# Gated attention on one core: the last MLP chunk's reads issued ahead of a load of x, and one gate value in another buffer

## The chip, the cores and the metric

The kernel runs on one core of a Trainium2 chip. A core has five engines that run side by side and wait for one another through semaphores: TensorE (matrix products, PE in the profile, its weight loads are PEld), VectorE (DVE), ScalarE (ACT), GpSimd (POOL) and SyncE (SP), which issues most of the DMAs. The metric is the time of one execution on the device in microseconds (us). Three executions of the kernel before took 1954.82, 1956.88 and 1960.61 us; the median is 1956.88.

## The reference

The input x has 2048 tokens of width 640. With a layer norm of it, attention and an MLP are computed side by side, and the MLP gates the attention:

```python
xn = layernorm(x)
q  = (xn @ wq)  per head                 # 32 heads of 128
p  = softmax(q @ k.T * 128**-0.5)        # the last 512 cached positions, no mask
s  = (p @ v, heads side by side) @ wo
h  = relu(xn @ w1 + b1) ** 2             # inner width 1728
g  = silu(h @ w2 + b2)
out = x + s * g
```

All arrays are float32, and the result has to be as exact as float32.

## The kernel before

**Products in three parts.** Each float32 operand is split into a high and a low part: ACT rounds a copy (`hi`), DVE or POOL subtracts (`lo`). A product is then three matmuls, high by high, high by low, low by high. In the profile a tile's split is a pair such as `ACT ACTIVATE ch<-ch` and `DVE TENSOR_TENSOR ch<-ch,ch`. A group of 15 matmuls is five such triples.

**Stages.** The tokens are cut into four tiles of 512. First comes the MLP: its inner width is 14 chunks (13 of 128 and one of 64). Tile 0 is done chunk by chunk; the first projections of tiles 1 and 2 are done next, and their activations are stored to DRAM as `h_m`. A loop over 28 steps then does the second projections of tiles 1 and 2, a chunk in each step (line 1275; steps 0 to 13 for tile 1, 14 to 27 for tile 2; below, chunk m is that of step m). The MLP of tile 3 is spread over the attention. Attention runs over 128 units (a token tile and a head each).

**One step of the loop.** `c_load(m + 3)` (line 764) reads a chunk's second weights (`cw`, 320 KB) and its activations (`ch<-h_m`, 256 KB) on SP's queue. `c_prep(m + 2, k)` (line 774) splits the activations (k = 0) and the weights (k = 1) on ACT and DVE. `c_down(m)` (line 801) is the step's 15 matmuls into five PSUM banks, `py`. The buffers are rings: four for raw weights (`wr`), four for raw activations (`tmp`), three for split weights, two for the split activations of odd steps. A tile that takes the next place in a ring waits for the last user of that place.

```python
for m in range(2 * FC):                      # line 1275, FC = 14
    t, f = CS[m]
    if m + 3 < 2 * FC:
        c_load(m + 3)
    if m + 2 < 2 * FC:
        for k in range(2):
            c_prep(m + 2, k)
    ...
```

**The border.** At step `OPEN` = 21 the attention's pool of tiles, `ep`, is opened, and the raw weights of head 0 (`qr`, `kr`) and the normalised x of the first token tile (`ax<-xT_d`, two DMAs of 1280 KB, high and low part) are read. At step 23 (`OPEN + 2`) head 0's weights are split, head 1's are read into the same single raw buffers, and the x of the second token tile is read into its own. At step 25 head 1's weights are split. At step 27, ahead of its 15 matmuls, TensorE does the first query projection (`pq`), which ACT and DVE turn into the first `q` value.

**The gate.** After the last step, `gate(T2, ...)` (line 520) makes tile 2's gate value from each of the five `py` banks: a sigmoid on ACT, a multiplication on DVE, and a store to DRAM on POOL's queue (`g_d<-sgl`). The function given to `gate` names the tile that holds the value. It is a tile of the tag `wv0` or `wv1`, in turn, the later home of the split v weights, each a ring of G = 2:

```python
gate(T2, lambda d: pools["ep"].tile([P, NT], F32, tag=f"wv{d % 2}", name=f"sgl{d}", bufs=G))
```

So values 0, 2 and 4 share the two places of `wv0`. TensorE meanwhile does 15 matmuls for tile 3 (`eu`), and then the first unit's scores (`s`, 12 matmuls), whose PSUM banks are those that `py` held. The scores of a unit are put at a fixed place in a block of 256 of TensorE's instructions (`align`, line 1373, first place 188), as are steps 4 to 20 of the loop (line 1315); padding instructions (NOP) fill up to it.

**The order of the work.** The code is unrolled. Instructions of PE, DVE, ACT, POOL and SP are in general kept in the order in which the code writes them on each engine, so what stands ahead on a queue and waits holds up what stands behind. From the attention's first unit on, a plan sorted by due times writes that order.

**Names in the profile.** Nearly every operation is recorded by one helper, so it shows line L77; the tile names tell them apart: `cw`, `ch` (second projection), `qr`, `kr`, `ax`, `pq`, `q` (query), `sgl`, `g_d` (gate), `eu` (tile 3's early projection), `s` (scores).

Of the kernel before, what the change touches and what calls it, by code (L numbers as in the profile page):

```python
# [8 lines left out]
F32 = mybir.dt.float32  # L9
# [5 lines left out]
P = 128  # L15
NT = 512
# [9 lines left out]
def kernel(  # L26
# [20 lines left out]
    DC = D // P  # L47
    FC = (F + P - 1) // P
    KC = W // P
    LATE = NTILE - 1  # L50
    OPEN = 2 * FC - 7
    SCALE = DH**-0.5
    G = 2
# [46 lines left out]
    T1, T2 = 1, 2  # L100
# [102 lines left out]
    def ln_chunk(t, c):  # L203
        if c == 0:
            open_x(t)
        bc, xs = LN[t], XS[t]
        xc = (
            pa.tile([P, D], F32, tag="xb", name=f"xc{t}_{c}", bufs=NB)
            if t == T2 and c in (1, 3)
            else xp.tile(  # L210
                [P, D], F32, tag="mr" if t == T2 and c == DC - 1 else "stage", name=f"xc{t}_{c}"
            )
        )[:, :NT]
        nc.sync.dma_start(xc, xT[c * P : (c + 1) * P, t * NT : (t + 1) * NT])
        dve.tensor_tensor(xc, xc, bc[0], op=ALU.subtract)
        dve.tensor_tensor(xc, xc, bc[1], op=ALU.mult)
        XC[t, c] = xc

    def ln_split(t, c, k):
        xc, xs = XC[t, c], XS[t]  # L220
        if k == 0:
            act.activation(xs[0][:, c, :], xc, AF.Copy)
        else:
            dve.tensor_tensor(xs[1][:, c, :], xc, raw(xs[0][:, c, :]), op=ALU.subtract)
# [135 lines left out]
    def spill(t, xs, cs=slice(0, DC)):  # L360
        for i in range(2):
            pool.dma_start(xT_d[t][i][:, cs, :], raw(xs[i])[:, cs, :])
# [144 lines left out]
    XS, HS, PY, LN, XC, WR, SUMS, TS, WB, PB, pools = ({} for _ in range(11))  # L507
# [12 lines left out]
    def gate(t, tiles, ds=range(DC)):  # L520
        for d in ds:
            py = PY[t][d]
            sg = tiles(d)
            act.activation(sg, py, AF.Sigmoid, bias=b2_sb[:, d : d + 1])
            dve.scalar_tensor_tensor(
                sg, py, b2_sb[:, d : d + 1], sg, op0=ALU.add, op1=ALU.mult
            )
            pool.dma_start(g_d[t][:, d, :], sg)
# [11 lines left out]
    def tmp(name):  # L540
        return xp.tile([P, NT], F32, tag="tmp", name=name, bufs=4)
# [222 lines left out]
    def c_load(m):  # L764
        t, f = CS[m]
        f0, n = chunks[f]
        r = xp.tile([P, D], F32, tag="wr", name=f"cw{m}", bufs=4)
        for i in range(0, P, n):
            sp.dma_start(r[i : i + n, :], w2[f0 : f0 + n, :])
        h = tmp(f"ch{m}")  # L770
        sp.dma_start(h[:n, :], h_m[t, f][:n, :])
        WR["c", m, 1], WR["c", m, 0] = r, h

    def c_prep(m, k):
        n = chunks[CS[m][1]][1]
        src = WR.pop(("c", m, k))
        if k:
            hi, lo = WB["c", m, 1] = [
                pc.tile([P, D], F32R, tag=f"w2{i}", name=f"cw{m}_{i}", bufs=3) for i in range(2)
            ]  # L780
        else:
            hs = (
                h_tiles(f"ch{m}")
                if m % 2
                else [
                    pc.tile([P, NT], F32R, tag="r", name=f"ch{m}_{i}", bufs=4) for i in range(2)
                ]
            )
            WB["c", m, 0] = hs[0] if n < P else hs
            hi, lo = (hs[0][:n, :], hs[0][n : 2 * n, :]) if n < P else hs  # L790
            src = src[:n, :]
        act.activation(hi, src, AF.Copy)
        dve.tensor_tensor(lo, src, raw(hi), op=ALU.subtract)
# [3 lines left out]
    def lead_slot(m):  # L797
        passes = sum(2 * (2 if chunks[CS[k][1]][1] < P else 3) * DC for k in range(LEAD_STEPS[0], m))
        return (MID_SLOT + passes + LEAD_PADS * (m - LEAD_STEPS[0])) % BLOCK

    def c_down(m):
        t, f = CS[m]
        if f == 0:
            PY[t] = [ps_y.tile([P, NT], F32, tag="py", name=f"py{t}_{d}") for d in range(DC)]
        down(f, WB.pop(("c", m, 1)), WB.pop(("c", m, 0)), PY[t])
# [14 lines left out]
    AHEAD = 2  # L820
# [12 lines left out]
    def open_xT(hf, t):  # L833
        XT[hf, t] = [
            pools["ep"].tile(
                [P, DC, NT], F32R, tag=f"x{i}", name=f"ax{hf}_{t}_{i}", bufs=TPH
            )
            for i in range(2)
        ]

    def load_xT(hf, t, i, cs, queue=sp):
        queue.dma_start(raw(XT[hf, t][i])[:, cs, :], xT_d[hf * TPH + t][i][:, cs, :])
# [12 lines left out]
    def load_raw(kind, hf, h):  # L855
        r = raw_tile(kind, f"{kind}r{hf}_{h}")
        src = {"q": wq, "k": kT, "v": v}[kind][h] if kind != "o" else wo[h * DH : (h + 1) * DH]
        if kind in "qv":
            r = r.rearrange("p (c d) -> p c d", d=DH)
        sp.dma_start(r, src)  # L860
        RAW[kind, hf, h] = r

    def prep(kind, hf, h, eng=None):
        shape = {"q": [P, DC, DH], "k": [P, W], "v": [P, KC, DH], "o": [P, D]}[kind]
        home = {"q": WQ, "k": KT, "v": VV, "o": WO}[kind]
        hi, lo = home[hf, h] = pair(f"w{kind}", shape, f"w{kind}{hf}_{h}", 2 * G if kind == "o" else G)
        src = RAW.pop((kind, hf, h))
        act.activation(hi, src, AF.Copy)
        (eng or pool).tensor_tensor(lo, src, raw(hi), op=ALU.subtract)

    def q_mm(i, cs):
        hf, g, t, h = units[i]
        if 0 in cs:
            QPS[i] = bank(f"pq{i}", 1)
        ws, xs = WQ[hf, h], XT[hf, t]
        for c in cs:
            triple(
                QPS[i],
                (ws[0][:, c, :], ws[1][:, c, :]),
                (xs[0][:, c, :], xs[1][:, c, :]),  # L880
                c == 0,
                c == DC - 1,
            )

    def q_hi(i):
        Q[i] = pair("q", [P, NT], f"q{i}", AHEAD + 1)
        act.activation(Q[i][0], QPS[i], AF.Copy, scale=SCALE)

    def q_lo(i):
        dve.scalar_tensor_tensor(  # L890
            Q[i][1], QPS.pop(i), SCALE, raw(Q[i][0]), op0=ALU.mult, op1=ALU.subtract
        )
# [381 lines left out]
    bctx.close()  # L1274
    for m in range(2 * FC):
        t, f = CS[m]
        if m + 3 < 2 * FC:
            c_load(m + 3)
        if m + 2 < 2 * FC:
            for k in range(2):  # L1280
                c_prep(m + 2, k)
        c, odd = divmod(m - 2, 2)
        if not odd:
            if 0 <= c < DC:
                ln_chunk(LATE, c)
                for k in range(2):
                    ln_split(LATE, c, k)
            if 0 < c <= DC:
                spill(LATE, XS[LATE], slice(c - 1, c))
        if m == OPEN:  # L1290
            pools["ep"] = ctx.enter_context(tc.tile_pool(name="early", bufs=1, side="right"))
            load_raw("q", 0, 0)
            load_raw("k", 0, 0)
            open_xT(0, 0)
            for i in range(2):
                load_xT(0, 0, i, slice(0, DC))
        if m == OPEN + 2:
            for kind in "qk":
                prep(kind, 0, 0, dve)
                load_raw(kind, 0, 1)  # L1300
            open_xT(0, 1)
            for i in range(2):
                load_xT(0, 1, i, slice(0, DC))
        if m == OPEN + 4:
            for kind in "qk":
                prep(kind, 0, 1, dve)
        if m == 2 * FC - 1:
            hctx.close()
            pools["psa"] = ctx.enter_context(
                tc.tile_pool(name="psa", bufs=1, space=PSUM, side="right")  # L1310
            )
            q_mm(0, range(DC))
            q_hi(0)
            q_lo(0)
        if m in LEAD_STEPS:
            pe.addr_align(BLOCK, lead_slot(m))
        c_down(m)
        if m == FC - 1:
            gate(T1, gate_tile)
    gate(  # L1320
        T2,
        lambda d: pools["ep"].tile([P, NT], F32, tag=f"wv{d % 2}", name=f"sgl{d}", bufs=G),
    )
    EARLY_IN = (-1,) * 5 + (0,) * 4 + (1,) * 4 + (2,) * 4 + (3,) * 3
    EARLY = [(FA + n // DC, n % DC) for n in range(len(EARLY_IN))]
    for (f, c), u in zip(EARLY, EARLY_IN):
# [127 lines left out]
    for item in order:  # L1454
        kind, n = item[0], int(item[1:] or 0)
# [125 lines left out]
```

## Time and profile before

| | |
|---|---|
| median of three executions | 1956.88 us |
| the profiled execution: time, span | 1955.08 us, 1953.3 us |
| TensorE busy | 1943.1 us (99%), 8576 matmuls |
| VectorE, ScalarE, GpSimd busy | 1599.5, 1242.6, 1348.2 us |
| granted TensorE clock | 0.999 |
| DMA traffic | 246.43 MB, mean 126 GB/s |

The span runs from the first to the last instruction of the profiled execution; its time has some 2 us around it. A row of a timeline gives start, length, engine, line, operation, tiles (output, arrow, inputs), shape and count; in brackets the idle time of the engine before it and what ended it. A row of the chain of waits gives start, length and what the end of the kernel waited for in that stretch. A row of waits gives who waited for whom, the total in us, how often, and the longest. A row of a stretch gives its bounds and length, the busy time of each engine (with the number of instructions), the granted clock, and the share and rate of the DMA engines. SPq and PEldq are the instruction queues of SyncE and TensorE.

### The profile page before, as it was taken

What the parts mean: (1) busy time and instruction counts of PE and PEld (TensorE: products, weight loads), DVE (VectorE), ACT (ScalarE), POOL (GpSimd) and SP (SyncE); (2) the same over time, 40 slices, a digit from 0 to 9 for tenths busy, and PEclk for the clock granted to TensorE, in tenths of its full rate; (3) what the DMA queues carried; (4) which work ended last, traced back from release to release, by engine and by line L of the source; (5) the groups of instructions that cost most, each with busy time, mean ns of one, the idle gap of its engine ahead of it and who ended that gap; (6) DMA issues with size and microseconds to landing.
All of it is one profiled execution on the core that took longest, in us unless ns stands there. A gap on an engine that the chain in (4) does not pass through costs nothing.

```text
span 1953.3 us, 28587 instructions
## 1 busy us (share of the span) xinstructions
PE 1943.1 (99%) x8576; PEld 1605.8 (82%) x8576; DVE 1599.5 (82%) x2758; ACT 1242.6 (64%) x2150; POOL 1348.2 (69%) x729
## 2 busy tenths in 40 slices
PE   9999999999999999999999999999999999999998
PEld 7888878888888888888888888888888888888887
DVE  6864747788888888888888878888888888888864
ACT  5665536766666666666666676666666666666643
POOL 1022106888888888888888888888888888888841
PEclk9999999999999999999999999999999999999999
DMA  7557953333332233333335433443343333323253
GB/s 267 150 179 252 365 176 112 98 93 92 93 92 93 92 93 92 93 93 92 92 98 179 144 110 109 114 114 114 114 114 114 114 114 114 98 92 93 85 186 119
DMA packets 147639, 246.43 MB, mean 126 GB/s; under 512 B 25020, under 2 KB 47334, under 8 KB 146214
## 3 DMA queue, kind: packets, MB, share of 16 engines
q1 hardware_dynamic: 144486, 230.02, 38.6%
q0 software_dynamic: 2864, 14.42, 1.8%
q8 instruction: 77, 1.26, 0.2%
q14 instruction: 68, 0.56, 0.1%
q10 hardware_dynamic: 144, 0.16, 0.0%
HBM read 213.59 MB, written 30.95 MB: 125 GB/s over the span
## 4 chain that ended last, share of the span: by engine, by line
PE 97%; DMA 2%; DVE 0%; issue 0%; ACT 0%; SPq 0%; ACTq 0%; POOLq 0%; DVEq 0%
PE r L77 22%; PE pq L77 22%; PE s L77 18%; PE o L77 18%; PE py L77 6%; PE ph L77 2%; PE ly L77 2%; PE wa L77 2%; PE lu L77 2%; PE wy L77 1%; PE wx L77 1%; DMA w1r<-in_w_dram 1%; DMA ch<-h_m 1%; PE eu L77 1%; DMA xb<-in_x_dram 0%; DMA w2r<-in_w_dram 0%
## 5 line engine op out<-in xcount | busy, mean ns | idle before, releaser
L77 POOL TENSOR_TENSOR pt<-e,pt 128x1024 fp32r<-128x1024 f32 x256 | 615.6, 2405 | 113.1 <-ACT pt L77 69.5
L77 PE MATMUL r<-ot,wo 128*128 128x512 f32 x1920 | 496.6, 389 | 0.0
L77 PE MATMUL pq<-ax,wq 128*128 128x512 f32 x1920 | 456.1, 389 | 0.0
L77 PEld LDWEIGHTS pq<-ax,wq 128*128 128x128 f32 x1920 | 360.4, 188 | 75.2 <-DVE q L77 0.4
L77 PEld LDWEIGHTS r<-ot,wo 128*128 128x128 f32 x1920 | 360.5, 188 | 74.7
L77 PE MATMUL s<-q,wk 128*128 128x512 f32 x1536 | 369.1, 389 | 1.4 <-DVE sgl L77 1.4
L77 PE MATMUL o<-pt,wv 128*128 128x512 f32 x1536 | 368.9, 389 | 0.0
L77 DVE TRANSPOSE_TENSOR_REDUCE rdm<-s 128x16 f32<-128x512 f32 x512 | 347.0, 712 | 6.3 <-PE s L77 5.3
L77 ACT ACTIVATE e<-e 128x1024 f32<-128x1024 f32 x256 | 269.8, 1054 | 123.1 <-DVE e L77 80.9
L77 PEld LDWEIGHTS s<-q,wk 128*128 128x128 f32 x1536 | 288.3, 188 | 61.5 <-DVE sgl L77 1.8
L77 PEld LDWEIGHTS o<-pt,wv 128*128 128x128 f32 x1536 | 288.4, 188 | 59.8
L77 DVE TENSOR_TENSOR e<-s,bm 128x512 f32<-128x512 f32 x512 | 312.6, 666 | 4.7 <-DMA bm<-m_d 4.1
L77 POOL TENSOR_TENSOR su<-e,e 128x1024 f32<-128x1024 f32 x128 | 309.1, 2415 | 0.0
L77 ACT ACTIVATE pt<-e 128x1024 fp32r<-128x1024 f32 x256 | 271.9, 1062 | 6.9
L77 ACT ACTIVATE rdm<-rdm 32x64 f32<-32x64 f32 x384 | 97.8, 255 | 183.5 <-DVE rdm L77 180.4
L77 DVE TENSOR_TENSOR acc<-r,acc 128x512 f32<-128x512 f32 x300 | 203.7, 679 | 12.9 <-PE r L77 12.5
L77 DVE TENSOR_TENSOR ot<-o,ot 128x512 fp32r<-128x512 f32 x128 | 88.5, 692 | 86.1 <-ACT ot L77 86.1
L77 DVE TRANSPOSE_TENSOR_REDUCE rds<-su 128x32 f32<-128x1024 f32 x128 | 158.3, 1237 | 0.2 <-POOL su L77 0.2
L77 ACT ACTIVATE q<-pq 128x512 fp32r<-128x512 f32 x128 | 76.7, 600 | 111.5 <-PE pq L77 111.5
L77 ACT ACTIVATE rds<-rds 32x32 f32<-32x32 f32 x384 | 89.7, 234 | 59.9 <-DVE rds L77 56.6
L77 POOL TENSOR_TENSOR wo<-or,wo 128x640 fp32r<-128x640 f32 x64 | 101.1, 1580 | 30.1 <-ACT wo L77 30.1
L77 POOL TENSOR_TENSOR wv<-vr,wv 128x512 fp32r<-128x512 f32 x64 | 83.3, 1301 | 52.1 <-ACT wv L77 45.3
(171 smaller groups left out, 2008.0 us busy)
## 6 DMA issues: line engine op xcount, KB each, us to landing
bm<-m_d SPq DMA_DIRECT2D x128, 256.0 KB, 3.2
bs<-s_d SPq DMA_DIRECT2D x128, 256.0 KB, 4.1
qr<-in_wq_dram SPq DMA_DIRECT2D x64, 320.0 KB, 4.3
or<-in_wo_dram SPq DMA_DIRECT2D x64, 320.0 KB, 4.7
kr<-in_kT_dram SPq DMA_DIRECT2D x64, 256.0 KB, 4.7
vr<-in_v_dram SPq DMA_DIRECT2D x64, 256.0 KB, 4.4
cw<-in_w_dram SPq DMA_DIRECT2D x26, 320.0 KB, 4.5
xT_d<-xT POOLq DMA_DIRECT2D x6, 1280.0 KB, 9.2
```

Source lines behind the costliest of these rows:

```text
L77: ins = method(*args, **kwargs)
```

## The change

Two edits. In the loop, step 23 issues the reads of chunks 26 and 27, and step 24 issues none; every other step is as before. So the two reads of chunk 27 stand in the code ahead of head 1's `qr` and `kr` and of the second token tile's two `ax`, and no longer behind them. And the fifth gate value of tile 2 (d = 4) takes a tile of the tag `q0`, the ring of three (`AHEAD + 1`) for the high parts of the `q` values, instead of the third turn in the ring `wv0`.

```diff
     for m in range(2 * FC):
         t, f = CS[m]
-        if m + 3 < 2 * FC:
-            c_load(m + 3)
+        for n in {OPEN + 2: (m + 3, m + 4), OPEN + 3: ()}.get(m, (m + 3,)):
+            if n < 2 * FC:
+                c_load(n)
         if m + 2 < 2 * FC:
...
-    gate(
-        T2,
-        lambda d: pools["ep"].tile([P, NT], F32, tag=f"wv{d % 2}", name=f"sgl{d}", bufs=G),
-    )
+    def sgl_tile(d):
+        tag, bufs = ("q0", AHEAD + 1) if d == DC - 1 else (f"wv{d % 2}", G)
+        return pools["ep"].tile([P, NT], F32, tag=tag, name=f"sgl{d}", bufs=bufs)
+
+    gate(T2, sgl_tile)
```

The two functions that are called with other arguments than before, `c_load` and the tile given to `gate`, stand in the code as follows:

```python
def c_load(m):                                            # line 764
    t, f = CS[m]
    f0, n = chunks[f]
    r = xp.tile([P, D], F32, tag="wr", name=f"cw{m}", bufs=4)
    for i in range(0, P, n):
        sp.dma_start(r[i : i + n, :], w2[f0 : f0 + n, :])
    h = tmp(f"ch{m}")                                     # tag "tmp", bufs=4
    sp.dma_start(h[:n, :], h_m[t, f][:n, :])
    WR["c", m, 1], WR["c", m, 0] = r, h

def gate(t, tiles, ds=range(DC)):                         # line 520
    for d in ds:
        py = PY[t][d]
        sg = tiles(d)
        act.activation(sg, py, AF.Sigmoid, bias=b2_sb[:, d : d + 1])
        dve.scalar_tensor_tensor(sg, py, b2_sb[:, d : d + 1], sg, op0=ALU.add, op1=ALU.mult)
        pool.dma_start(g_d[t][:, d, :], sg)
```

## The prediction

> **What bounds the kernel now.** I read the page first: busy shares and the chain that ended last.
>
> ```profile
> span 1953.3 us, 28587 instructions
> PE 1943.1 (99%) x8576; PEld 1605.8 (82%) x8576; DVE 1599.5 (82%) x2758; ACT 1242.6 (64%) x2150; POOL 1348.2 (69%) x729
> ...
> PE 97%; DMA 2%; DVE 0%; issue 0%; ACT 0%; SPq 0%; ACTq 0%; POOLq 0%; DVEq 0%
> ```
>
> TensorE sets the end almost everywhere, so a change pays only what it closes between two matmuls. Second view: TensorE's waits between 31 us (end of the start-up) and 1947 us. There are two, and both lie at the border that the change touches.
>
> ```profile
> PE s L77 <- DVE sgl L77: 1.4, 1, 1.4
> PE py L77 <- ACT cw L77: 0.7, 1, 0.7
> ```
>
> Third view: TensorE's timeline over the border. Groups in order: first query projection (`pq`), the last chunk's second projection (`py`), an early first projection of the last token tile (`eu`), the first scores (`s`), the next query projection.
>
> ```profile
> 280.69 3.56 PE L77 MATMUL pq<-ax,wq 128*128 128x512 f32 x15
> 284.99 4.12 PE L77 MATMUL py<-ch,cw 128*128 128x512 f32 x15 [0.74 <-ACT cw L77]
> 288.95 3.56 PE L77 MATMUL eu<-xT,w1s 128*128 128x512 f32 x15
> 293.87 3.06 PE L77 MATMUL s<-q,wk 128*128 128x512 f32 x12 [1.36 <-DVE sgl L77]
> 296.77 0.62 PE L77 MATMUL pq<-ax,wq 128*128 128x512 f32 x2
> ```
>
> Fourth view: the chain of waits over the border. It shows what stands behind the two waits.
>
> ```profile
> 271.83 11.77 DMA ch<-h_m
> ...
> 288.92 3.32 DMA g_d<-sgl
> ...
> 293.07 0.76 DVE sgl L77
> ...
> 293.87 3.06 PE s L77 x12
> 296.93 3.17 PE pq L77 x14
> ```
>
> Two DMAs: the read of the last chunk's activations (`ch`, chunk 27 of 0 to 27), which takes 11.77 us, and the store of the first gate value (`g_d<-sgl`), whose landing frees the buffer that the fifth gate value wants.
>
> **Part 1: the last chunk's reads go ahead of the second token tile's x.** Today's order on SP's queue:
>
> ```profile
> 258.87 0.43 SPq L77 DMA_DIRECT2D ch<-h_m  x1
> 269.43 0.33 SPq L77 DMA_DIRECT2D qr<-in_wq_dram  x1
> 270.03 0.33 SPq L77 DMA_DIRECT2D kr<-in_kT_dram  x1
> 270.42 0.90 SPq L77 DMA_DIRECT2D ax<-xT_d  x2
> 271.36 0.43 SPq L77 DMA_DIRECT2D cw<-in_w_dram  x1
> 271.83 0.43 SPq L77 DMA_DIRECT2D ch<-h_m  x1
> ```
>
> The first row is the second of chunk 26's two reads. Head 1's `qr` has one buffer and waits until VectorE has split head 0's; chunk 27 stands behind it and behind 2.5 MB of `ax`. In the new order chunk 27's two DMAs come straight after chunk 26's. Their own condition is a free buffer, chunk 23's, which the split of chunk 23's weights on VectorE gives back (chunk 26's read went out as chunk 22's split ended, one step earlier):
>
> ```profile
> 261.04 0.82 DVE L77 TENSOR_TENSOR cw<-cw,cw 128x640 fp32r<-128x640 f32 x1 [1.97 <-ACT cw L77]
> ```
>
> So they are issued at about 261.04 + 0.82 = 261.9 and 262.3 instead of 271.36 and 271.83. What the queue does in those stretches, with the landing times of `ch` reads issued from 240 to 262 us:
>
> ```profile
> 262.00:269.00 7.00, 7.00 (x33) 5.79 (x32) 3.06 (x5) 3.19 (x6) 0.00 (x0) 1.00 0.01 4
> 272.50:283.60 11.10, 11.10 (x50) 9.19 (x49) 0.00 (x0) 0.00 (x0) 0.00 (x0) 1.00 0.78 283
> DMA to landing us min/median/max: 3.2/3.4/3.6
> ```
>
> Nearly nothing moves from 262 to 269 (4 GB/s), so the read lands at 262.3 + 3.4 = 265.7, not 283.6. The moved DMAs pass `qr`, `kr` and two `ax` on SP and nothing on POOL. Cost for those four: nothing, since SP sits idle from 259.3 to 269.43 and the reads end before; if that cover failed, they would move by one issue pair (0.33 + 0.43 = 0.8 us), and `ax` serves the second tile's projection, which starts here:
>
> ```profile
> 302.89 3.56 PE L77 MATMUL pq<-ax,wq 128*128 128x512 f32 x15
> ```
>
> What is late next for chunk 27? The splits on ACT and DVE today, and after:
>
> ```profile
> 270.47 0.74 ACT L77 ACTIVATE cw<-cw 128x640 fp32r<-128x640 f32 x1 [0.99 <-PE py L77]
> 283.68 0.63 ACT L77 ACTIVATE ch<-ch 128x512 fp32r<-128x512 f32 x1 [12.48 <-DMA ch<-h_m]
> 284.22 0.72 ACT L77 ACTIVATE cw<-cw 128x640 fp32r<-128x640 f32 x1
> ```
>
> ACT takes `ch` at 270.47 + 0.74 = 271.2. The weights' split goes to a buffer that chunk 24's matmuls free one step (3.40 us) after the row above: 273.9. With DVE's 0.82 behind ACT's 0.74 all is split by 275.5, some 8.6 us before TensorE wants it at 280.69 + 3.40 = 284.09 (15 matmuls take 3.40: the 14 of the chain's last row take 3.17, 0.227 each). Head 1's splits follow and leave the busy stretch 284.8 to 287.1, so the gate values no longer queue behind them.
>
> Gain, by starts: `pq` to `py` takes 284.99 − 280.69 = 4.30 for 3.40 of work, lost 0.90; `py` to `eu` takes 288.95 − 284.99 = 3.96, lost 0.56 (the weights' low part came later still). Together 1.46. Between nothing and 1.46 I take 1.46, as the margin is 8.6 us.
>
> **Part 2: the fifth gate value goes to a buffer of q.** Today's gate values:
>
> ```profile
> 286.48 2.69 ACT L77 ACTIVATE sgl<-py,b_sb 128x512 f32<-128x512 f32 x4
> 292.35 0.69 ACT L77 ACTIVATE sgl<-py,b_sb 128x512 f32<-128x512 f32 x1 [3.18 <-DMA g_d<-sgl]
> ```
>
> The fifth shares a ring of two buffers with the first and third. It waits 3.18 us for the first's store, then costs 0.69 on ACT and 0.76 on DVE (the chain's 293.07 row), and the scores' banks (the five `py` banks) come free only then. In a ring of three q buffers, of which only the first is taken, nothing has to land. After part 1, `py` runs 284.09 to 287.49; its last bank ends near 287.7 (0.389 for the last matmul, which starts at 287.26), ACT follows to 288.4, DVE to 289.2. `eu` occupies TensorE until 287.49 + 3.40 = 290.89, so 1.7 us are left and the wait is gone. Lost today: `eu` to `s` 293.87 − 288.95 = 4.92 for 3.40, 1.52; `s` to `pq` 296.77 − 293.87 = 2.90 for 12 × 0.227 = 2.72, 0.18 (a restart). Together 1.70.
>
> What the borrowed buffer adds: the third q value takes the first's place in the ring instead of a fresh one, and the fourth waits for the fifth gate value's store. When they are written:
>
> ```profile
> 306.59 0.57 ACT L77 ACTIVATE q<-pq 128x512 fp32r<-128x512 f32 x1
> 314.33 0.60 ACT L77 ACTIVATE q<-pq 128x512 fp32r<-128x512 f32 x1 [1.92 <-PE pq L77]
> DMA to landing us min/median/max: 2.3/5.0/5.1
> ```
>
> The first q value is read last by the scores that end by 297, 9 us before 306.59; the store is issued near 289 and lands within 5.1 us, 20 us before 314.33. Cost nothing. If either cover failed, what queues behind that ACT copy is the exponential of the same unit, and TensorE behind it; the nearest row for such a wait is the 3.18 above. The v weights' ring has one user less: looser.
>
> Sum: 0.90 + 0.56 + 1.52 + 0.18 = 3.16 us; as a check, 57 matmuls from 280.69 end at 293.61, where the row says 296.77. The profiled execution took 1955.08 (span 1953.3), 1.8 under the median of the three runs, 1956.88; it would become 1951.9, and the median 1956.88 − 3.16 = **1953.7**.
>
> [...]
>
> **Rivals.**
> [...]
> 2. *The reads do not move.* SP's queue need not follow the code: the first `qr` is written after chunk 24's reads, yet it was issued early, among those of chunks 10 and 11:
>
> ```profile
> 207.46 0.56 SPq L77 DMA_DIRECT2D ch<-h_m  x1
> 208.19 0.33 SPq L77 DMA_DIRECT2D qr<-in_wq_dram  x1
> ```
>
>    It opened a new pool, which the second `qr` does not. Then only part 2 acts: the fifth value follows the fourth on ACT at 286.48 + 2.69 = 289.17 and leaves DVE at 289.17 + 0.69 + 0.76 = 290.6, or one 0.76 later behind the fourth; `eu` ends at 288.95 + 3.40 = 292.35, so gain 1.7: 1955.2. Chance 0.06.
> 3. *A wait takes the place of the gate's.* If the q buffer is not free at once, the fifth value waits for the first's store as now: the first bank ends at 284.09 + 0.68 + 0.16 = 284.9, ACT and DVE make it 286.4, the store lands 3.32 later at 289.8, and the fifth value is done at 291.2, 0.3 after TensorE is ready. Gain 2.9: 1954.0; with a landing as slow as 5.1 it is 1.8 worse, gain 1.1: 1955.8. Chance 0.08.
> 4. *Slower: the padding of TensorE's code overflows.* The scores must begin at a fixed place in a block of 256 instructions, and padding fills up to it. Between the last aligned chunk step and the scores stand these:
>
> ```profile
> L77 PEldq NOP  x3: 13/13/13, 288.3 to 288.5; - x3
> L77 PEldq EVENT_SEMAPHORE  x2: 51/51/51, 276.6 to 276.7; - x2
> ```
>
>    Only three pads are left. With more than three further wait instructions in this stretch the padding wraps by 256. The 18 pads behind the scores' start took 1.3 us, 0.07 each:
>
> ```profile
> L77 PEldq NOP  x18: 13/13/13, 293.9 to 295.2; - x18
> ```
>
>    The three pads now stand at 288.3, behind `eu` in the stream; with `py` 0.9 earlier, 253 more from about 287.4 on take 18 us and end near 305, and the scores come 11 us later than now: 1968. Against it: the matmuls of this stretch wait for the same engines as before, and I find no reason for even one more. Chance 0.04.
>
> **How the numbers follow.** Forecast 0.80, rivals 0.02, 0.06, 0.08, 0.04. The forecast's own range: the three runs span 1954.82 to 1960.61, from −2.1 to +3.7 about their median, and a median of runs scatters some 2 to 3 us. Added to 1953.7, and drawn up to take in rivals 2 and 3, this gives 1950.4 to 1957.4. About 0.3% (5.9 us) is what a measurement of this kernel can tell from no change. No stall in this trace is worth that: faster needs 2.7 us of scatter on top or rival 1, 0.10; slower is rival 4 and a share for a wait I do not see, 0.06; within, 0.84.
>
> **What would show it.** In the changed kernel: chunk 27's `cw` and `ch` on SP near 262, ahead of `qr`; no wait of ACT for `ch`; `py` 3.40 after the first `pq`; five gate values in one row on ACT; `s` 3.40 after `eu`, and 6.80 after `py` instead of 293.87 − 284.99 = 8.88; TensorE's two waits gone from its list. Wrong would be: a landing of `ch` later than 275, a gap ahead of `s` with another releaser, or more than three pads ahead of it.

## The result and the profile after

The changed kernel's median is **1953.14 us** (15 executions, 1952.38 to 1956.56) against 1956.88 for the kernel before (15 executions, 1954.24 to 1960.61). The ratio is 0.9982 with a 95% interval of 0.9974 to 0.9990: 0.18% faster, between 0.10 and 0.26%, and so inside the 0.3% that the prediction called no change. It had said 1953.7.

The page of the profiled execution (time 1952.56 us), with the shares of its chain of work:

```profile
span 1950.8 us, 28585 instructions
PE 1941.4 (100%) x8576; PEld 1604.7 (82%) x8576; DVE 1600.1 (82%) x2758; ACT 1242.5 (64%) x2150; POOL 1347.4 (69%) x729
...
PE 98%; DMA 1%; DVE 0%; ACT 0%; SPq 0%; issue 0%
```

TensorE's share of the chain rises from 97 to 98%, that of DMA falls from 2 to 1%. Between 31 and 1947 us the list of waits has no row for TensorE any more; before it had two. The border on TensorE's timeline (start, length, engine, operation, tiles, count):

```profile
281.36 3.56 PE L77 MATMUL pq<-ax,wq 128*128 128x512 f32 x15
284.76 3.56 PE L77 MATMUL py<-ch,cw 128*128 128x512 f32 x15
288.16 3.56 PE L77 MATMUL eu<-xT,w1s 128*128 128x512 f32 x15
291.56 2.88 PE L77 MATMUL s<-q,wk 128*128 128x512 f32 x12
294.28 3.56 PE L77 MATMUL pq<-ax,wq 128*128 128x512 f32 x15
```

The starts stand 3.40, 3.40, 3.40 and 2.72 apart, which is 57 matmuls without a gap. From `pq` to `pq` it is 294.28 − 281.36 = 12.92 us; before it was 296.77 − 280.69 = 16.08. The difference is **3.16 us**. The span fell by 1953.3 − 1950.8 = 2.5 only, because the first `pq` of this execution began 281.36 − 280.69 = 0.67 later, and 3.16 − 0.67 is 2.5. The start-up differs from execution to execution, whatever the change: near 30 us TensorE waits for `w1s`, not at all in the first profile of the kernel before, 1.3 us in its second, and up to 1.6 us in the profiles of the other kernels. Against the median, 3.16 is 0.16%, inside the interval. Behind each step, SP's queue, ACT and DVE (timelines; a bracket gives the idle time ahead and what ended it):

```profile
259.54 0.43 SPq L77 DMA_DIRECT2D ch<-h_m  x1
262.56 0.33 SPq L77 DMA_DIRECT2D cw<-in_w_dram  x1
262.94 0.43 SPq L77 DMA_DIRECT2D ch<-h_m  x1
270.09 0.33 SPq L77 DMA_DIRECT2D qr<-in_wq_dram  x1
...
271.08 0.90 SPq L77 DMA_DIRECT2D ax<-xT_d  x2
```

```profile
271.78 0.62 ACT L77 ACTIVATE ch<-ch 128x512 fp32r<-128x512 f32 x1
...
285.64 3.41 ACT L77 ACTIVATE sgl<-py,b_sb 128x512 f32<-128x512 f32 x5
```

```profile
275.31 0.82 DVE L77 TENSOR_TENSOR cw<-cw,cw 128x640 fp32r<-128x640 f32 x1 [1.98 <-ACT cw L77]
...
286.37 3.47 DVE L77 SCALAR_TENSOR_TENSOR sgl<-py,b_sb,sgl 128x512 f32<-128x512 f32 x5
```

Chunk 27's reads go out at 262.56 and 262.94, ahead of `qr`; ACT takes `ch` at 271.78 without waiting; the last split ends at 275.31 + 0.82 = 276.13, 8.6 before `py`. The five gate values are one row of five on ACT and on DVE, and the last ends at 286.37 + 3.47 = 289.84, 1.7 before the scores. The chain of waits holds TensorE alone where two DMAs stood:

```profile
281.52 3.40 PE pq L77 x15
284.92 3.40 PE py L77 x15
288.32 3.40 PE eu L77 x15
291.72 2.72 PE s L77 x12
```

### The profile page after: what moved, and what is told of

Same layout as the page of the kernel before. It is cut to its first block, busy times and chain, and to the rows that moved or that the text cites. A ratio compares the mean times of both kernels' runs of the same rounds, so it can differ in the third digit from the quotient of the medians.

```text
span 1950.8 us, 28585 instructions
## 1 busy us (share of the span) xinstructions
PE 1941.4 (100%) x8576; PEld 1604.7 (82%) x8576; DVE 1600.1 (82%) x2758; ACT 1242.5 (64%) x2150; POOL 1347.4 (69%) x729
## 4 chain that ended last, share of the span: by engine, by line
PE 98%; DMA 1%; DVE 0%; ACT 0%; SPq 0%; issue 0%
PE pq L77 22%; PE r L77 22%; PE o L77 18%; PE s L77 18%; PE py L77 7%; PE ph L77 2%; PE ly L77 2%; PE wa L77 2%; PE lu L77 2%; PE wy L77 1%; PE wx L77 1%; PE eu L77 1%; DMA w1r<-in_w_dram 1%; DMA xb<-in_x_dram 0%; DMA w2r<-in_w_dram 0%; DVE acc L77 0%
```

## The experiments

The sum came out, so what is open is whether its parts are what the prediction said: 1.46 us from part 1 (the reads) and 1.70 from part 2 (the gate value), independent of each other. The rival reading: the late read also delayed the gate values, so that part 1 alone closes most of both stalls. Below, "border" is the time from the first `pq` to the next on TensorE, 16.08 before and 12.92 after. All these kernels compute the whole result.

### Part 1 alone, twice

The kernel before with the first of the two edits, the loop that issues the reads; the fifth gate value stays in the ring of two.

> Part 1 alone: chunk 27's reads ahead of the second token tile's x, the fifth gate value still third in the ring of two. Theory A (the two stalls are separate costs that add, 1.46 and 1.70 us): 1.5 us less than the kernel before, the scores' first matmul still 4.9 us after the first eu matmul. Theory B (both hang on the late read; the gate's wait shrinks when the first gate value's store goes out earlier): the first store is issued near 286.5, lands 3.3 us later, and the scores begin 0 to 0.5 us after TensorE is ready, so 2.7 to 3.1 us less than before; with a landing of 5.1 us the gap is 2 us and the gain 1.1.

TensorE, ACT and DVE at the border of this kernel:

```profile
282.42 3.56 PE L77 MATMUL pq<-ax,wq 128*128 128x512 f32 x15
285.82 3.56 PE L77 MATMUL py<-ch,cw 128*128 128x512 f32 x15
289.22 3.56 PE L77 MATMUL eu<-xT,w1s 128*128 128x512 f32 x15
292.62 3.01 PE L77 MATMUL s<-q,wk 128*128 128x512 f32 x12
295.47 3.56 PE L77 MATMUL pq<-ax,wq 128*128 128x512 f32 x15
```

```profile
286.70 2.73 ACT L77 ACTIVATE sgl<-py,b_sb 128x512 f32<-128x512 f32 x4
291.10 0.69 ACT L77 ACTIVATE sgl<-py,b_sb 128x512 f32<-128x512 f32 x1 [1.66 <-DMA g_d<-sgl]
```

```profile
291.82 0.75 DVE L77 SCALAR_TENSOR_TENSOR sgl<-py,b_sb,sgl 128x512 f32<-128x512 f32 x1 [1.60 <-ACT sgl L77]
```

The next `pq` starts at 295.47, so the border is 13.05: part 1 alone gains **3.03 of the 3.16 us**. The fifth gate value still waits for the first's store, but DVE ends it at 291.82 + 0.75 = 292.57, and the scores start at 292.62: just in time. Its start on ACT moved from 292.35 − 280.69 = 11.66 behind the first `pq` to 291.10 − 282.42 = 8.68, and the 2.98 between them have two sources. The first store is issued 6.28 behind `pq` (288.70) and not 8.23 (288.92), 1.95 less: 0.90 because `py` starts that much sooner, the rest because ACT and DVE no longer split chunk 27 and head 1's weights just ahead of the gate. And the store lands in 2.29 us instead of 3.32. The median was 1953.98 (10 executions) against 1956.17 (25), ratio 0.9990 (0.9980 to 0.9999). That is 2.2 us less, but anything from 0.2 to 3.9 by the interval, so the 1.46 of part 1 would fit it too; what decides is the timeline.

The 13.05 stood on a margin of 0.05, so the same kernel was run once more:

> Part 1 alone, profiled once more. In its first profile the first gate value's store landed 2.3 us after its issue and the scores began 3.40 us after eu, with no wait. If that holds in general (the splits out of the way let the store go out early, and the v weights' read starts 0.7 us behind it), the gap is again 0 to 0.2 us. If the landing was lucky and can be 3.3 to 5.1 us, a gap of 0.9 to 2.7 us is back ahead of the scores.

It took 1954.35 us (one execution; the kernel before beside it 1955.35). Border 295.52 − 282.44 = 13.08, ACT's wait 1.68, landing 2.30: the same picture. The theory that the two parts add up falls, in both timelines.

### Part 2 alone, twice

The kernel before with the second edit, the fifth gate value in a buffer of `q`; the reads stay where they were.

> Part 2 alone: the fifth gate value in a buffer of q, the reads of chunk 27 still behind the x. Theory A and B alike: ch still lands near 283.6, py still begins 0.9 us late and runs 3.96 us, but the gap ahead of the scores (1.52 and 0.18 us) is gone: 1.7 us less than before. If the fifth value still ends after eu (DVE busy with the fourth), a few tenths of the gap stay.

TensorE and ACT:

```profile
281.23 3.56 PE L77 MATMUL pq<-ax,wq 128*128 128x512 f32 x15
284.63 3.74 PE L77 MATMUL py<-ch,cw 128*128 128x512 f32 x15
288.21 3.56 PE L77 MATMUL eu<-xT,w1s 128*128 128x512 f32 x15
```

```profile
282.95 0.63 ACT L77 ACTIVATE ch<-ch 128x512 fp32r<-128x512 f32 x1 [11.21 <-DMA ch<-h_m]
```

Median 1954.17 (10 executions), ratio to before 0.9989 (0.9980 to 0.9998). The next `pq` starts at 294.33, border 13.10. In this execution `ch` reached ACT 1.72 behind the start of `pq` (282.95 − 281.23); before it was 2.99 (283.68 − 280.69). So only 0.18 was lost within `py`, and the reads' stall is nearly absent although nothing was done about it. To see which is usual, the same kernel and the kernel before were profiled again:

> Part 2 alone, profiled once more. In the first profile of it ch landed 1.7 us after pq began and py had no gap ahead of it. If that was chance, a second execution shows another landing, and with one 3.0 us after pq began the 0.90 and 0.56 us at py are back; the scores in any case start 3.4 us after eu.

```profile
281.64 3.56 PE L77 MATMUL pq<-ax,wq 128*128 128x512 f32 x15
285.79 4.09 PE L77 MATMUL py<-ch,cw 128*128 128x512 f32 x15 [0.59 <-ACT cw L77]
289.72 3.56 PE L77 MATMUL eu<-xT,w1s 128*128 128x512 f32 x15
293.12 2.88 PE L77 MATMUL s<-q,wk 128*128 128x512 f32 x12
```

Part 2 alone again, 1954.26 us: the stall ahead of `py` is back, the one ahead of `s` is gone, and with the next `pq` at 295.84 the border is 14.20. Here part 2 gains 1.9, near the 1.7 of rival 2.

> The kernel before, profiled once more, unchanged. If the two stalls are fixed costs, the gaps are again 0.90 and 0.56 us at py and 1.52 us ahead of the scores (first pq to next pq 16.1 us). If they hang on how long the read of ch takes behind the x, they move with it: each us by which ch lands earlier takes as much off the stall at py, down to none when ch lands less than about 2 us after the first pq matmul starts.

```profile
282.32 3.56 PE L77 MATMUL pq<-ax,wq 128*128 128x512 f32 x15
286.55 4.11 PE L77 MATMUL py<-ch,cw 128*128 128x512 f32 x15 [0.67 <-ACT cw L77]
...
295.29 3.01 PE L77 MATMUL s<-q,wk 128*128 128x512 f32 x12 [1.23 <-DVE sgl L77]
```

The kernel before, 1956.42 us, has both stalls again, border 298.14 − 282.32 = 15.82. So without part 1 the loss ahead of and within `py` varies between the four profiles: 0.18, 1.28, 1.38 and 1.46 us. It goes with how long ACT waits for `ch`: 11.21, 12.33, 12.40 and 12.48 us. Why one execution got it 1.1 us sooner stays open.

### The reads between SP's wait and x

Chunk 27 stood behind two things on SP: head 1's `qr`, which waits for a buffer, and the 2.5 MB of x. This kernel has both parts, but puts the reads behind the `qr` and `kr` and ahead of `ax` alone:

```diff
+        if m + 3 < 2 * FC and m != OPEN + 3:
             c_load(m + 3)
...
                 load_raw(kind, 0, 1)
+            c_load(m + 4)
             open_xT(0, 1)
```

> Both parts, but chunk 27's reads stand behind head 1's q and k weights on SP's queue and ahead of the x alone. It parts two causes of the late read: the SP queue's wait for head 0's split (until 269.4) and the 2.5 MB of x ahead in the DMA rings. If the x is the cause, ch is issued near 270.9, lands 3.3 to 5 us later (by 276), and no gap is left: the same 3.2 us less than before as the changed kernel. If the queue's wait is the cause, ch lands near 283 and the gap of 0.9 us ahead of py returns.

TensorE, SP's queue and ACT:

```profile
282.43 3.56 PE L77 MATMUL pq<-ax,wq 128*128 128x512 f32 x15
...
295.35 3.56 PE L77 MATMUL pq<-ax,wq 128*128 128x512 f32 x15
```

```profile
272.62 0.42 SPq L77 DMA_DIRECT2D ch<-h_m  x1
273.09 0.90 SPq L77 DMA_DIRECT2D ax<-xT_d  x2
```

```profile
277.81 0.63 ACT L77 ACTIVATE ch<-ch 128x512 fp32r<-128x512 f32 x1 [4.87 <-DMA ch<-h_m]
```

`ch` is issued at 272.62, 9.81 ahead of `pq` at 282.43; before it was 271.83, 8.86 ahead. That is 0.95 earlier and no more. But ACT has it 277.81 − 272.62 = 5.2 us after the issue and not 11.85 (283.68 − 271.83), and there is no gap: the border is 295.35 − 282.43 = 12.92, the median 1953.01 (10 executions; ratio 0.9987, 0.9978 to 0.9997), that of the changed kernel. So the transfers of x ahead of the read made it late; SP's wait, which is still there, costs nothing by itself. Whether ending that wait alone, with x still ahead, would have helped too was not tried.

### A second chunk behind x

The opposite dose: the kernel before, with chunk 26's reads too moved behind x.

```diff
-        if m + 3 < 2 * FC:
+        if m + 3 < 2 * FC and m != OPEN + 2:
             c_load(m + 3)
...
                 load_xT(0, 1, i, slice(0, DC))
+            c_load(m + 3)
```

> The kernel before with one more chunk behind the x: the reads of chunk 26 too are issued after the second token tile's x. If a read behind 2.5 MB of x lands some 11.8 us after its issue and TensorE pays what is not covered, chunk 26's ch lands near 283.3 and its split ends near 285, where its matmuls would have begun at 277.4: a gap of about 7.5 us ahead of them; chunk 27's stall (1.46) vanishes behind it, so 6 us more than before (1962). If such reads are covered (ACT and DVE catch up, or the DMA rings serve them between the x), no difference.

TensorE, and busy times by stretch (TensorE, its weight loads, DVE, ACT, POOL; then granted clock, DMA share, GB/s):

```profile
285.52 6.11 PE L77 MATMUL py<-ch,cw 128*128 128x512 f32 x15 [7.62 <-ACT cw L77]
291.47 3.56 PE L77 MATMUL pq<-ax,wq 128*128 128x512 f32 x15
```

```profile
277.80:285.40 7.60, 0.11 (x1) 0.00 (x0) 0.52 (x1) 1.19 (x2) 0.00 (x0) 0.67 0.71 287
285.40:291.40 6.00, 5.88 (x15) 4.50 (x16) 3.72 (x6) 2.47 (x5) 0.00 (x0) 0.56 0.00 0
291.40:301.70 10.30, 10.30 (x48) 8.31 (x46) 4.23 (x6) 4.02 (x6) 2.16 (x4) 1.00 0.28 80
```

1962.62 us (5 executions) against 1956.06 (16), ratio 1.0031 (1.0017 to 1.0044). TensorE stands still for 7.6 us while the DMA engines are 71% busy, and the 15 matmuls behind the gap take 291.47 − 285.52 = 5.95 instead of 3.40, at a granted clock of 0.56. Gap and slow matmuls together are 10.2 us. The border's own stalls are gone in exchange (`pq` to `s` is 301.68 − 291.47 = 10.21, without a gap), about 3 us, which leaves some 7; the medians differ by 6.6.

### The padding made to overflow, and filled to the last place

Rival 4 said that more than three further instructions ahead of the scores would wrap the padding by 256. The changed kernel, with step 21 pushed back by four pads:

```diff
+        if m == OPEN:
+            pe.addr_align(BLOCK, lead_slot(m) - LEAD_PADS + 4)
         c_down(m)
```

> The changed kernel with step 21 of the loop put on a place 4 pads further, so that the stretch up to the first scores holds one instruction too many and the padding ahead of the scores wraps to 255. Theory of the prediction (a pad costs 0.07 us of TensorE's queue and little of it is hidden): 18 us of pads, the scores begin near 305 instead of 291.6, 13 to 14 us slower than the changed kernel, about 10 us slower than before. If the queue of matmuls ahead hides them: up to 18 us less than that, no difference from the changed kernel.

```profile
287.32 3.56 PE L77 MATMUL eu<-xT,w1s 128*128 128x512 f32 x15
305.46 4.71 PE L77 MATMUL s<-q,wk 128*128 128x512 f32 x12 [14.57 <-issue]
310.00 2.20 PE L77 MATMUL pq<-ax,wq 128*128 128x512 f32 x9
```

```profile
290.80:305.40 14.60, 0.09 (x1) 0.00 (x0) 0.00 (x0) 0.69 (x1) 0.00 (x0) 0.66 0.18 71
305.40:310.00 4.60, 4.54 (x12) 3.65 (x13) 1.91 (x3) 0.00 (x0) 0.00 (x0) 0.59 0.01 4
```

1969.64 us (4 executions), ratio to before 1.0074 (1.0058 to 1.0091), 16.5 above the changed kernel. The scores come at 305.46. Counted from the start of `eu` they are 305.46 − 287.32 = 18.14 behind instead of 3.40: 14.74 late. The missing 1.8 is again the clock: 12 matmuls take 310.00 − 305.46 = 4.54 instead of 2.72, at 0.59. With three instead of four in the same line:

> The changed kernel with step 21 put 3 pads further, one less than in the run whose padding wrapped. The three pads ahead of the scores are used up exactly: no pad is left, nothing wraps, and the time and the border (12.9 us from the first pq to the next) are those of the changed kernel. If moving step 21 itself cost something, some of the 16 us of that run would be seen here too.

1952.47 us (one execution; the kernel before beside it 1955.35), border 294.15 − 281.23 = 12.92: no cost. The threshold lies where the three pads said.

### A later stall, taken by itself

With the border closed, the next loss behind it is of 0.32 us, at the fourth `pq`: it starts 0.19 late and takes 3.53 instead of 3.40. It waits for the low part of the third `q` value on DVE. The changed kernel, with that low part due earlier in the plan:

```diff
-            qs = [(1, 2.8, 4.1), (2, 9.1, PERIOD - 5.2)]
+            qs = [(1, 2.8, 4.1), (2, 9.1, 5.5)]
```

> The changed kernel with the third q value's low part placed between the third and fourth max-fold of the second unit on VectorE instead of behind them. The one stall left after the border (0.30 us at the fourth q projection, released by VectorE's q) should go: 0.3 us less in the trace, too little for the timed runs to tell. Rival: the fourth fold comes 0.65 us later and with it the row of maxima, the shift and the exponentials, and TensorE waits as long at a later place.

The median was 1952.59 (11 executions; ratio to before 0.9983, 0.9974 to 0.9992). From the first scores to the fourth `pq` it now takes 307.26 − 290.94 = 16.32, against 308.07 − 291.56 = 16.51 in the changed kernel, and the group itself takes 3.40. But further on 0.4 us is lost again: by the first `r` group this kernel is 46.77 from its first scores, the changed one 46.56. No gain can be claimed, and the median's interval is nearly that of the changed kernel.

## Why the prediction was right, and where it was not

**The bound and the sum: right.** TensorE sets the end, both stalls went, nothing came in their place: 0.90 + 0.56 + 1.52 + 0.18 = 3.16 was predicted and 16.08 − 12.92 = 3.16 measured. The median fell by 3.74, within its interval of 2.0 to 5.1 (0.10 and 0.26% of 1956.88).

**Part 1's steps: right.** The predicted times, moved by the 0.67 of the later start-up: reads issued 262.6 and 263.0 (measured 262.56 and 262.94), splits done 276.2 (276.13), margin 8.6 (8.6). `qr`, `kr` and `ax` lost nothing by being passed. Whether x delayed the read or SP's wait ahead of x, the prediction left undivided; the kernel with the reads between the two shows that passing x is enough.

**Part 2's steps as they stand behind part 1: right.** Fifth value done at 289.87 by the same count (289.84), slack 1.7 (1.7). The covers of the q ring held: the third and fourth `q` copies on ACT wait for no DMA, so the borrowed buffer cost nothing.

**The step that failed: "Lost today ... together 1.70", credited to part 2.** The two stalls do not add up as two parts, each with its own. The prediction saw that after part 1 the gate values no longer queue behind the splits, and did not carry it into this term: the store goes out 1.95 us earlier, and the fifth gate value is then in time even with its wait. Its own rival 3 had worked that out, but for a failing of part 2 and not as what part 1 is worth alone. Part 1 alone gains 3.0; part 2 on top of it gains 0.13, the restart of the scores (13.05 against 12.92). Part 2 alone gains 1.9 to 3.0, and then part 1 has the rest to give. The total does not depend on this, so the forecast stood, but whoever had kept part 1 alone by those terms would have expected 1.46 us of it where the border closes by 3.03 (1955.4 and 1953.9, counted from 1956.88). The medians of the parts alone (1953.98, 1954.17) and of both (1953.14, 1953.01 with the reads between `kr` and `ax`) lie too close to rank them, the more so as the start-up alone moves the first `pq` between 280.52 and 282.44 in these profiles; that they differ rests on the timelines.

**The range.** 1950.4 to 1957.4 held the median with room on both sides; the 15 executions of the changed kernel lie between 1952.4 and 1956.6.

**The rivals.**
1. More idle time freed than the two gaps (chance 0.02): no. The border is all that closed. The weight loads' share of the span did not follow the gaps: it stayed at 82% (1605.8 us before, 1604.7 after) while TensorE's waits between 31 and 1947 us vanished.
2. The reads do not move: they moved, by 8.8 to 8.9 us on SP. Its price for part 2 alone, 1.7, was met by one execution (1.9) and passed by another (3.0), since the stall ahead of `py` varies.
3. A wait takes the place of the gate's: not in the changed kernel. But part 1 alone is this rival's case, as its fifth value must wait for the first's store, and the 2.9 priced there came out as 3.03. It was near by luck, as two errors met: the store went out 0.6 later than assumed (2.88 behind the start of `py`, priced 2.3) and landed 1.0 sooner (2.29 against 3.32).
4. The padding: not here, but real. It was priced at 1968 with the scores near 305; forced, it gave 1969.6 and 305.5. The surplus is near the 1.8 us that the 12 score matmuls took longer at a granted clock of 0.59, which the prediction had not seen.

## What to carry to other kernels

Two stalls that stand one behind the other at a border may have one cause: before crediting each to its own edit, move the first and follow every engine that it held up to the second. Where a chain needs a small read soon, try it ahead of a large load on the same queue; here being ahead of 2.5 MB of x was what counted (5.2 us from issue to ACT instead of 11.85), not being early (it was issued 0.95 us earlier). Where instructions are padded to fixed places, count the pads that are left: here three were the distance between no cost and 16 us.

## What the runs showed of the hardware

**The two long gaps cost more than their length.** Behind gaps of 7.6 and 14.6 us the granted clock was 0.56 and 0.59 (the stretches above), and the first 15 or 12 matmuls took 5.95 and 4.54 us instead of 3.40 and 2.72: 2.5 and 1.8 us on top. Over the gaps themselves it was 0.67 and 0.66, so it had fallen before the matmuls began. In the next stretches, 291.40 to 301.70 and 310.00 to 330.00, it was 1.00 again. The gaps of the kernel before, 0.7 and 1.4 us, left the clock at 1.00:

```profile
285.00:289.00 4.00, 3.87 (x16) 2.88 (x17) 4.00 (x8) 4.00 (x7) 0.08 (x1) 1.00 0.00 0
289.00:294.00 5.00, 3.64 (x17) 2.71 (x16) 2.13 (x4) 1.43 (x3) 2.08 (x4) 1.00 0.79 270
```

Behind 31 us the lists of TensorE's waits have no gap between 1.6 and 7.6 us, so the length from which a gap lowers the clock was not shown.

**The read behind 2.5 MB of x landed late.** In the kernel before, `ch` landed 3.2 to 3.6 us after its issue where it was issued from 240 to 262 us, and 11.77 us after it behind 2.5 MB of x. In the kernels that left it there ACT waited 11.2 to 12.5 us for it, and where it was 11.2 TensorE lost 0.18 us. Whether the read would have been spared on another queue was not tried.

**The gate's first store** landed in 3.32 and 3.18 us in the two profiles of the kernel before, where SP issued the next read (`vr`) 0.2 us behind it, and in 2.29 and 2.30 with part 1 alone, where that read came 0.7 behind. Whether the read is the reason was not tried.
